# Attention and Fourier mixing on one core: first loads shared out anew, copies of values by engines in place of transfers, and a new order of work

## The chip, the cores and the metric

The kernel runs on one core of a Trainium2 chip. The core has a matrix engine (TensorE, PE in the profile), three engines for elementwise work (VectorE or DVE, ScalarE or ACT, GpSimd or POOL) and SyncE (SP), which only issues transfers. Transfers are issued by SyncE and ScalarE on two hardware queues, and by GpSimd on a software queue, which can change a type from fp32 to fp16 on the way. The metric is device time in microseconds: 255.69 us, the median of three runs (255.09, 255.69 and 258.91).

## The reference

Attention over four batches, eight heads, 768 positions, 64 columns, with a distance penalty and a narrow mask, then Fourier mixing over positions and columns, a normalisation and two feed-forward products:

```python
scores = q @ k.T / 8 - slope[h] * dist           # keys 0..7 for all, else 0 <= i - j < 96
a = exp(scores - max) / sum
x = (a @ v), heads side by side                  # 4 x 768 x 512
u = x + real(fft(fft(x, axis=1), axis=2))
un = (u - mean(u)) / sqrt(var(u) + 1e-6)
out = u + max(un @ w_ch1, 0) @ w_ch2             # 512 -> 2048 -> 512
```

## The kernel before

**Batches and stages.** Each batch goes through four stages. Attention works on pairs of heads: pairs 0 to 3 belong to batch 0, 4 to 7 to batch 1, and so on. q and k of a pair are turned so that the head's columns lie on partitions (`trans`, TensorE, for batches 0 and 1; transposing transfers, `trans_dma`, for 2 and 3). Scores come in three groups of blocks (`score`), ScalarE takes the exponential, the weighted sums with the values follow (`av`), and VectorE divides by the row sum (`norm`). In batches 0 and 1 the distance penalty is a product as well: `score` first multiplies the distance table `dist_sb` (in the tile `misc`) by a scaled identity, L676, and adds q·k on top, L690. In batches 2 and 3 a mask `mk` is multiplied in afterwards, L725. Folds of x, products with tables (`y_unit`, `u_unit`) and a sum make u; each batch has three units of two row groups, c = 0 to 11, and each unit is normalised (`centre`), transposed (`nt_unit`), and sent through the products with w_ch1 (`ph_unit`, L1292) and w_ch2 (`pg_unit`, `pg_units`, L1325 and L1434).

**Two kinds of copies.** A block's scores need the keys of its own and of the block before, and key blocks 1 to 4 exist a second time with the first 16 rows of each half taken from block 0, the global keys. `swap` in `trans` makes that copy for batches 0 and 1 (the tile kB, which lies in `mk`; L630 and L631). The values have the same: vB holds value blocks 1 to 4 with the first rows taken from block 0. `v_back`, L731 to L748, makes vB for each pair. For batches 0 and 1 it is a copy of the whole, 128x528, and two copies of 16 rows, 16x528, on GpSimd or VectorE. For batches 2 and 3 (`b >= FB`) it is three transfers on SyncE's queue: rows 32 to 127 (L739) and twice rows 0 to 31 (L741). There are eight pairs in batches 2 and 3, so 24 such transfers. `av` waits for vB.

**First loads.** Pair 0 (`load_qk` with `n in pl.HW`) is read in four halves as fp32 by the hardware queues, 192 KB each, into the tile u, and cast to fp16 into hT by ScalarE or VectorE (L544, L546). Everything else of q, k and v comes by GpSimd's queue with the cast on the way. GpSimd's queue, and the hardware queues together, hold eight transfers in flight each; a ninth issue waits until the first has landed. `dma_const` reads the identity, 32 KB, and the distance table, 320 KB, on a hardware queue.

**The order.** The order of the work on every engine is written out by hand as lists of names, `Plan.ORDER`, L197: A, M, H and G are units of TensorE work (attention, mixing, first and second feed-forward product), `A9.0` is the first follow-up of unit A9, and `T.17` is the seventeenth piece that no unit makes, transfers for the most part. `Plan.run` goes through the lists, and the semaphores follow from what each piece reads and writes. An engine works strictly down its list: what stands behind a waiting piece waits too. So the order before of the first loads is: ScalarE's queue takes the distance table, both halves of k, the first half of q; SyncE's takes the second half of q and the identity; GpSimd's takes q and k of pairs 2 and 3, then values, then pair 1.

Of the kernel before, what the change touches and what calls it, by code (L numbers as in the profile page):

```python
# [14 lines left out]
P = 128  # L15


class Ring(str):

    k = 0  # L20
# [4 lines left out]
class Plan:  # L25
# [112 lines left out]
    def move(self, go=False):  # L138
# [3 lines left out]
        both = [h[2] for k, h in act if k != "AQ"]  # L142
        each = sum(both) * (self.MIX if len(both) > 1 else 1.0) / 1000.0
        rate = {k: h[2] / 1000.0 if k == "AQ" else each for k, h in act}
# [31 lines left out]
    def unit_start(self, unit):  # L176
# [7 lines left out]
        if not there:  # L184
# [7 lines left out]
    AQ = ()  # L192
# [14 lines left out]
        ),  # L207
        "ACT": (
# [9 lines left out]
        ),  # L218
        "DVE": (
# [11 lines left out]
        ),  # L231
        "POOL": (
# [5 lines left out]
        ),  # L238
# [5 lines left out]
        ),  # L244
    }

# [60 lines left out]
def kernel(  # L307
# [22 lines left out]
    FB = 2  # L330
# [1402 lines left out]
```

## Time and profile before

| | |
|---|---|
| runs | 255.09, 255.69, 258.91 us |
| the profiled execution | 253.6 us, its span 251.5 us |
| mean granted TensorE clock | 0.991 of full speed |
| busy: TensorE, VectorE, ScalarE, GpSimd | 233.2, 196.0, 129.9, 105.5 us |
| GpSimd's queue (q0) | 66,176 packets, 17.06 MB |
| SyncE's queue (q1) | 30,128 packets, 13.15 MB |
| ScalarE's queue (q10) | 3,712 packets, 3.28 MB |

The views: *windows* give, for stretches of the span, its length, then for each engine busy microseconds and instructions, the granted clock (PEclk), the share of transfer engines and GB/s. *Timeline* rows have the start, the busy time, the engine, the line, the operation, the tile written and read, and in brackets how long the engine had been idle and what ended that. `ACTq` or `SPq` is an instruction of the engine's sequencer, here one that issues a transfer. Views of a line or tile give minimum, median and maximum duration in nanoseconds and the first and last start. A TensorE row's busy time has modelled ends, so units that run into each other look full even where they wait a little.

### The profile page before, as it was taken

To read this page: it belongs to the slowest core of one execution; us is meant where nothing else is said; L and a number is where in the kernel's file an instruction comes from. 1 tells how busy PE (TensorE), PEld (TensorE's weight loads), DVE (VectorE), ACT (ScalarE), POOL (GpSimd) and SP (SyncE) were. 2 spreads that over 40 slices of the span, in tenths; PEclk is the share of its full clock that TensorE was granted. 3 is DMA by queue.
4 is the path that set the end of the run, shared out by engine and by line. 5 is a ranking of instruction groups with operands and counts; after the bars stand their busy time and mean duration, and the time that the engine had idled before them with its cause. 6 is when DMAs were issued, how large, how long until landed. Compare 5 with 4: busy or idle time off the path is not lost.

```text
span 251.5 us, 7622 instructions
## 1 busy us (share of the span) xinstructions
PE 233.2 (93%) x3251; PEld 192.0 (76%) x3251; DVE 196.0 (78%) x425; ACT 129.9 (52%) x216; POOL 105.5 (42%) x151
## 2 busy tenths in 40 slices
PE   7468698899999999999999999999999999999994
PEld 2356586678756766788887978899889888888883
DVE  1255899987976669999998977789978987575683
ACT  2039568665559665754646568484436603204300
POOL 8689996999124922929801002220030160001210
PEclk9889999999999999999999999999999999999998
DMA  7999999999999998999999990230651222030412
GB/s 177 177 156 136 164 166 234 199 198 145 173 183 192 182 178 174 128 196 119 135 192 244 232 165 5 86 89 0 169 209 44 42 42 86 0 44 1 169 67 100
DMA packets 100049, 33.96 MB, mean 135 GB/s; under 512 B 86736, under 2 KB 96592, under 8 KB 100016
## 3 DMA queue, kind: packets, MB, share of 16 engines
q0 software_dynamic: 66176, 17.06, 69.6%
q1 hardware_dynamic: 30128, 13.15, 24.8%
q10 hardware_dynamic: 3712, 3.28, 4.8%
q8 instruction: 25, 0.41, 0.7%
q14 instruction: 8, 0.07, 0.1%
HBM read 31.48 MB, written 8.65 MB: 160 GB/s over the span
## 4 chain that ended last, share of the span: by engine, by line
PE 57%; DVE 6%; SPq 2%; DMA 2%; POOL 1%; issue 1%; ACT 0%; DVEq 0%; POOLq 0%
PE ph L1292 25%; PE pgD L1434 12%; PE pgA L1434 9%; PE pg L1325 4%; PE pav L774 2%; PE sc L684 2%; PE py L1057 2%; DMA out_dram<-u 2%; PE pu L1145 1%; DVE u L1452 1%; DVE u L1197 1%; SPq L578 1%; DVE sb L1410 1%; SPq L741 0%; SPq L739 0%
## 5 line engine op out<-in xcount | busy, mean ns | idle before, releaser
L1292 PE MATMUL ph<-unT,w 128*128 128x256 f16 x768 | 94.3, 273 | 0.6 <-ACT hT L1298 0.5
L1292 PEld LDWEIGHTS <-w 128*128 128x128 f16 x768 | 73.7, 98 | 11.7 <-issue 0.9
L1298 ACT ACTIVATE hT<-ph 128x512 f16<-128x512 f32 x71 | 41.4, 596 | 59.5 <-PE ph L1292 59.4
L1238 POOL TENSOR_SCALAR sm<-sm 128x2 f32<-128x2 f32 x12 | 4.0, 331 | 93.9 <-ACT un L1231 93.5
L1434 PEld LDWEIGHTS <-hT 128*128 128x128 f16 x320 | 30.9, 98 | 4.0
L710 ACT ACTIVATE er<-sc 128x1024 f16<-128x1024 f32 (+1 forms) x24 | 22.7, 953 | 11.9 <-PE sc L684 8.6
L713 ACT ACTIVATE ex<-sc 128x1024 f16<-128x1024 f32 (+1 forms) x24 | 21.7, 967 | 13.4 <-PE sc L690 13.4
L1299 DVE TENSOR_SCALAR hT<-ph 128x512 f16<-128x512 f32 x25 | 16.9, 685 | 9.7 <-PE ph L1292 9.6
L1452 DVE SCALAR_TENSOR_TENSOR u<-pgA,sm,u 128x256 f32<-128x256 f32 (+1 forms) x30 | 17.0, 567 | 5.5 <-PE pgA L1434 5.0
L725 DVE TENSOR_TENSOR ex<-er,mk 128x1024 f16<-128x1024 f16 (+1 forms) x24 | 15.0, 640 | 5.1 <-ACT er L710 4.5
L499 POOL DMA_DIRECT2D qk<-in_k_dram x16 | 13.6, 867 | 10.3 <-DMA qkT<-qk 9.1
L1452 DVE SCALAR_TENSOR_TENSOR u<-pgD,sm,u 128x512 f32<-128x512 f32 (+1 forms) x21 | 15.1, 721 | 3.0 <-PE pgD L1434 1.8
L1325 PE MATMUL pg<-w,hT 128*128 128x512 f16 x64 | 15.6, 379 | 0.0
L1231 ACT ACTIVATE un<-un 128x512 f16<-128x512 f16 x24 | 14.9, 625 | 0.1
L774 PE MATMUL pav<-v,ex 128*128 128x65 f16 x224 | 13.2, 193 | 1.5 <-DVE qkT L623 1.0
L1071 ACT ACTIVATE zy<-py 128x512 f16<-128x512 f32 (+1 forms) x13 | 10.2, 793 | 8.4 <-PE py L1057 6.7
L774 PEld LDWEIGHTS <-ex 128*128 128x128 f16 x352 | 12.3, 97 | 2.7 <-issue 1.3
L499 POOL DMA_DIRECT2D qk<-in_q_dram x16 | 13.6, 857 | 0.6 <-DMA v<-in_v_dram 0.5
L786 DVE TENSOR_TENSOR x<-pav,rc 128x384 f16<-128x384 f32 x24 | 12.6, 554 | 0.6
L1057 PE MATMUL py<-t,ww 128*128 128x256 f16 x80 | 11.0, 272 | 0.5 <-ACT ex L713 0.5
L1239 POOL TENSOR_TENSOR sm<-sm,mhalf 128x2 f32<-128x2 f32 x12 | 10.6, 887 | 1.0
L676 PE MATMUL sc<-misc 64*64 64x512 f16 (+1 forms) x96 | 9.4, 372 | 1.8 <-ACT qkT L626 0.8
(166 smaller groups left out, 467.9 us busy)
## 6 DMA issues: line engine op xcount, KB each, us to landing
w<-in_moe_w_ch_dram POOLq DMA_DIRECT2D x8, 512.0 KB, 9.3
out_dram<-u SPq DMA_DIRECT2D x15, 256.0 KB, 2.6
v<-in_v_dram POOLq DMA_DIRECT2D x12, 192.0 KB, 7.1
qk<-in_k_dram POOLq DMA_DIRECT2D x16, 96.0 KB, 5.2
qk<-in_q_dram POOLq DMA_DIRECT2D x16, 96.0 KB, 5.4
xr<-xd SPq DMA_DIRECT2D x3, 512.0 KB, 5.2
xd<-x ACTq DMA_DIRECT2D x2, 768.0 KB
vB<-v SPq DMA_DIRECT2D x8, 99.0 KB, 3.6
```

Of the source, the lines that this page charges most:

```text
L499: nc.gpsimd.dma_start(qk16[n][:, w, :, h], src[b, h0 + h].rearrange("(i m) d -> m i d", m=P))
L710: A(mine(), cut(pa), AF.Exp, 0.0, 0.125)
L713: A(cut(expst[hp][:, :, g * 512:g * 512 + (384 if g == 2 else 512)]), cut(pa), AF.Exp, 0.0, 0.125)
L725: VT(o, mine(), m, op=ALU.mult)
L774: nc.tensor.matmul(o[:, s * 65:(s + 1) * 65], lhsT, w, start=(a == 0), stop=(a == len(ops) - 1), skip_group_check=True)
L1057: nc.tensor.matmul(o, lhsT, rhs, start=(x == 0), stop=(x == len(ops) - 1))
L1292: nc.tensor.matmul(ph[:, a * CH:(a + 1) * CH].rearrange("p (x m) -> p x m", x=2), W1[0][:, d, jb * P:(jb + 1) * P], UNT[c][:, :, d, :], st ...
L1298: pl.later([("ACT", act(512), lambda: A(dst, ph, AF.Relu)), ("DVE", dve(512), lambda: V.tensor_scalar_max(dst, ph, 0.0))], [], e, [("h", c ...
L1299: ("DVE", dve(512), lambda: V.tensor_scalar_max(dst, ph, 0.0))],
L1325: nc.tensor.matmul(pg, HT[c][:, jb, t * P:(t + 1) * P], W2[0][:, jb, :], start=(jb == 0), stop=(jb == NJ - 1))
L1434: nc.tensor.matmul(o, lhs(j), rhs(j), start=(first and j == 0), stop=(j == NK - 1), skip_group_check=True)
L1452: V.scalar_tensor_tensor(o, x, r(t), acc, op0=ALU.mult, op1=ALU.add)
```

## The change

1. **First halves.** The order puts the second half of k and the first half of q on SyncE's queue; ScalarE's takes the second half of q, the identity and the first half of k. ScalarE casts three halves and VectorE one (before: two and two).
2. **Distance table.** `dma_const` gets a third way for the table, GpSimd's queue, and the order uses it: fifth there, behind q and k of pairs 2 and 3. Behind it come k of pair 1 and the values of pairs 0 and 2.
3. **vB of batches 2 and 3.** The transfers are gone. One whole copy and one copy of 32 rows, on GpSimd (pairs 1 and 2 of batch 2, all four of batch 3) or VectorE (pairs 0 and 3 of batch 2). `av` no longer waits for the second and third transfer.
4. **Order made anew.** All five lists are new. Among what moves until the first unit is transposed: TensorE starts with the scores of pair 0 in place of pair 2's. The key copies of pairs 0, 2 and 5 go from VectorE to GpSimd, those of pairs 3 and 1 the other way; that of pair 0 stands behind GpSimd's thirteenth load, that of pair 2 behind two loads more. Two of the three copies of spread rows (L1129) go from VectorE to ScalarE (L1127), and the copy of pair 6's transposed q and k from ScalarE (L626) to VectorE (L623). VectorE's division for the last pairs of batch 1 comes after the first unit's transposition, and so do two more of the weighted sums of batch 1 on TensorE. On SyncE's queue the table for the masks stands behind a transposing transfer of batch 2 in place of one of the vB transfers.

The planner's own estimates in `move` and the costs in `later` change as well; with the order written out, they decide nothing of the program that is built.

```diff
@@ Plan.move
-        both = [h[2] for k, h in act if k != "AQ"]
+        sw = any(k == "SW" for k, h in act)
+        both = [h[2] for k, h in act if k != "AQ" or sw]
...
-        rate = {k: h[2] / 1000.0 if k == "AQ" else each for k, h in act}
+        rate = {k: h[2] / 1000.0 if k == "AQ" and not sw else each for k, h in act}
@@ Plan.ORDER, the heads of the lists
         "PE": (
-            "A0 A1 A5 A15 A9 A8 A19 A20 A18 A4 A6 A2 A3 A14 A13 A10 A12
+            "A0 A5 A1 A15 A3 A2 A4 A7 A20 A6 A9 A8 A10 A19 A11 A12 A14
...
         "ACT": (
-            "T.9 T.6 T.4 T.0 T.7 T.5 A9.0 A19.0 A20.0 A18.0 A8.0 A4.0
+            "T.2 T.8 T.4 T.7 T.1 T.5 A3.0 A4.0 A2.0 A7.0 A20.0 A8.0
...
         "POOL": (
-            "T.11 T.12 T.20 T.19 T.16 T.21 T.13 T.23 T.36 T.18 T.14 T.32 T.15 T.17 T.33 A15.0
+            "T.11 T.12 T.19 T.20 T.9 T.14 T.15 T.16 T.18 T.13 T.17 T.21 T.22 A1.0 T.36 T.31 T.30 A5.0
...
         "SP": (
-            "T.2 T.8 T.131 T.35 T.10
+            "T.6 T.0 T.136 T.35 T.10
@@ v_back
-        if b >= FB:
-            low, high = slice(0, 32), slice(32, P)
-            pl.later([("SP", 0.66, lambda: nc.sync.dma_start(vB[hp][high], v16[b % 2][high, h, 1:NS - 1, :]))], after, 0.0, [("vB", b, hp)], lat=0.5, dma=(192, 1.56))
-            for x in range(2):
-                pl.later([("SP", 0.66, lambda x=x: nc.sync.dma_start(vB[hp][low, x], head(low)[:, x]))], after, 0.0, [("vC", b, hp, x)], lat=0.5, dma=(128, 0.6))
-            return
+        rows = (slice(0, 32),) if b >= FB else (slice(0, GR), slice(64, 64 + GR))
 
         def cp(eng):
             eng.tensor_copy(vB[hp], v16[b % 2][:, h, 1:NS - 1, :])
-            for r in (slice(0, GR), slice(64, 64 + GR)):
+            for r in rows:
                 eng.tensor_copy(vB[hp][r], head(r))
@@ av
-            needs = [...] + VN(b, [hp]) + [("vB", b, hp)] + [("vC", b, hp, z) for z in range(2 * (b >= FB))]
+            needs = [...] + VN(b, [hp]) + [("vB", b, hp)]
@@ dma_const
         ways = both(lambda on: on.dma_start(dst, src.ap()), 0.48 if soon else 0.42)
+        if tok == ("c", "dist"):
+            ways = ways + [("POOL", 0.66, lambda: nc.gpsimd.dma_start(dst, src.ap()))]
```

More of the change, by code (lines that the diff above doesn't have):

```diff
@@ L198 @@
         "PE": (
[8 rows of a table removed]
[8 rows of a table added]
         ),
         "ACT": (
[9 rows of a table removed]
[9 rows of a table added]
         ),
         "DVE": (
[11 rows of a table removed]
[11 rows of a table added]
         ),
         "POOL": (
[5 rows of a table removed]
[5 rows of a table added]
         ),
         "SP": (
[4 rows of a table removed]
+            "T.6 T.0 T.136 T.35 T.10 T.127 T.133 T.128 T.130 T.134 T.91 G7.1 G3.1 T.137 T.131 T.100 T.101 T.176 T.185 T.205 T.102 T.177 T.206 T.182 T.34 "
+            "T.140 T.186 T.211 T.212 T.183 T.149 T.179 T.180 T.150 T.151 T.223 T.189 T.222 T.229 T.228 T.198 T.199 T.239 T.200 T.240 T.246 T.245 T.256 "
+            "T.258 T.257 "
         ),
@@ L736, in v_back @@
         after = VN(b, [hp]) + [("sets",)] + [("avh", b - 1, hp)] * (b > 0)
-        if b >= FB:
-            low, high = slice(0, 32), slice(32, P)
-            pl.later([("SP", 0.66, lambda: nc.sync.dma_start(vB[hp][high], v16[b % 2][high, h, 1:NS - 1, :]))], after, 0.0, [("vB", b, hp)], lat=0.5, dma=(192, 1.56))
-            for x in range(2):
-                pl.later([("SP", 0.66, lambda x=x: nc.sync.dma_start(vB[hp][low, x], head(low)[:, x]))], after, 0.0, [("vC", b, hp, x)], lat=0.5, dma=(128, 0.6))
-            return
+        rows = (slice(0, 32),) if b >= FB else (slice(0, GR), slice(64, 64 + GR))
         def cp(eng):
             eng.tensor_copy(vB[hp], v16[b % 2][:, h, 1:NS - 1, :])
-            for r in (slice(0, GR), slice(64, 64 + GR)):
+            for r in rows:
                 eng.tensor_copy(vB[hp][r], head(r))
-        pl.later([("POOL", 1.8, lambda: cp(nc.gpsimd)), ("DVE", 0.9, lambda: cp(V))], after, 0.0, [("vB", b, hp)], rank=RA(b))
+        pl.later([("POOL", 0.6 + 0.6 * len(rows), lambda: cp(nc.gpsimd)), ("DVE", 0.3 + 0.3 * len(rows), lambda: cp(V))], after, 0.0, [("vB", b, hp)], rank=RA(b))
     def v_global(b):
@@ L807, in av @@
         for x in range(1 if b else 2):
-            needs = [("ex", b, hp, g) for g in ((0, 1, 2) if b else (1, 2) if x else (0, 1))] + VN(b, [hp]) + [("vB", b, hp)] + [("vC", b, hp, z) for z in range(2 * (b >= FB))]
+            needs = [("ex", b, hp, g) for g in ((0, 1, 2) if b else (1, 2) if x else (0, 1))] + VN(b, [hp]) + [("vB", b, hp)]
             needs += [("av", b - 1, g, 0) for g in range(HP) if b > FB] + [("qkT", HP + g) for g in range(2) if b == 1] + [("av", b, hp, 0)] * x
```

70 rows, old and new, of the table ORDER are left out of this document.

## The prediction

> **What bounds the kernel now.** I read the windows first, cut where the work changes its kind, then the transfers of the first 15 us, then the timeline of the first 25 us.
>
> ```profile
> core 0: us, PE busy (x) PEld busy (x) DVE busy (x) ACT busy (x) POOL busy (x), PEclk, DMA share, GB/s
> 0.00:6.33 6.33, 4.88 (x15) 1.75 (x15) 0.86 (x2) 1.81 (x2) 5.25 (x11) 1.00 0.80 178
> 6.33:10.02 3.69, 0.00 (x1) 0.00 (x0) 0.41 (x3) 0.52 (x1) 1.92 (x6) 1.00 1.63 185
> 10.02:14.59 4.57, 3.99 (x73) 3.58 (x73) 2.84 (x11) 0.00 (x0) 3.33 (x5) 0.64 2.11 165
> 14.59:20.00 5.41, 3.82 (x130) 2.91 (x128) 1.36 (x4) 3.24 (x4) 5.35 (x8) 0.99 2.51 149
> 20.00:30.00 10.00, 7.91 (x226) 6.27 (x221) 7.42 (x17) 7.16 (x9) 9.16 (x14) 1.00 2.27 153
> 30.00:45.80 15.80, 12.60 (x318) 9.77 (x318) 15.37 (x44) 12.00 (x19) 13.61 (x21) 1.00 1.51 196
> 45.80:56.20 10.40, 9.67 (x192) 7.93 (x192) 8.98 (x21) 7.25 (x11) 10.00 (x17) 1.00 1.47 196
> 56.20:80.00 23.80, 23.11 (x276) 16.89 (x275) 19.88 (x43) 15.01 (x29) 10.48 (x16) 1.00 1.48 175
> 80.00:245.00 165.00, 164.37 (x2011) 140.66 (x2010) 136.67 (x283) 82.93 (x145) 46.38 (x61) 1.00 0.71 115
> ```
>
> From 80 to 245 us TensorE stands still for 0.63 us of 165, and from 56.2 to 80 for 0.69. Its work is the same after the change, so time is gained or lost only where TensorE idles: before 56.2 us, and in a tail whose order is unchanged. Before 10.02 us there is no useful work at all (the x15 are warm-up products); between 30 and 45.8 us VectorE, busy 15.37 of 15.8, is the bound.
>
> ```profile
> GB/s 0 0 0 0 55 123 298 292 285 324 337 329 270 193 160 152 210 210 199 191 182 176 185 165 179 180 178 164 159 157 156 173 176 167 157 155 159 171 176 159
> ...
> hT<-in_k_dram POOLq DMA_DIRECT2D x3, 192.0 KB, 8.6
> ...
> u<-in_k_dram ACTq DMA_DIRECT2D x2, 192.0 KB, 6.4
> misc<-distm ACTq DMA_DIRECT2D x1, 320.0 KB, 3.4
> ...
> ident<-idm SPq DMA_DIRECT2D x1, 32.0 KB
> ```
>
> The transfers of the first 15 us: bandwidth in 40 slices of 0.375 us, then issues with their size and median time to landing. It runs at some 300 GB/s until 4.9 us, then 155 to 210, for good. Summed, 2313 × 0.375 = 867 KB have moved by 4.9 us.
>
> ```profile
> 4.71 0.37 DVE L546 CAST hT<-u 128x384 f16<-128x384 f32 x1 [3.31 <-DMA u<-in_q_dram]
> ...
> 5.46 0.52 ACT L544 ACTIVATE hT<-u 128x384 f16<-128x384 f32 x1 [1.33 <-DMA u<-in_k_dram]
> ...
> 8.19 0.52 ACT L544 ACTIVATE hT<-u 128x384 f16<-128x384 f32 x1 [2.21 <-DMA u<-in_k_dram]
> 9.61 0.36 DVE L546 CAST hT<-u 128x384 f16<-128x384 f32 x1 [4.52 <-DMA u<-in_q_dram]
> ...
> 10.02 2.56 PE L599 MATMUL pt<-ident,hT 128*64 128x128 f16 x48 [3.69 <-DVE hT L546]
> 10.07 0.75 POOL L482 DMA_DIRECT2D v<-in_v_dram  x1 [1.81 <-DMA hT<-in_q_dram]
> ...
> 11.18 0.83 POOL L539 DMA_DIRECT2D hT<-in_k_dram  x1 [0.37 <-DMA hT<-in_k_dram]
> ...
> 13.17 1.06 PE L599 MATMUL pt<-ident,hT 128*64 128x128 f16 x16 [0.58 <-DMA hT<-in_q_dram]
> ...
> 14.59 0.39 PE L676 MATMUL sc<-misc 64*64 64x384 f16 x4
> ...
> 15.20 0.81 ACT L713 ACTIVATE ex<-sc 128x768 f16<-128x768 f32 x1 [6.49 <-PE sc L690]
> ...
> 16.07 0.63 POOL L630 COPY mk<-qkT 128x512 f16<-128x512 f16 x1
> 16.76 0.29 POOL L631 COPY mk<-qkT 128x128 f16<-128x128 f16 x1
> ...
> 17.57 7.72 ACT L713 ACTIVATE ex<-sc 128x1024 f16<-128x1024 f32 x9 [1.56 <-PE sc L690]
> ```
>
> The last q half, fourth on ScalarE's queue behind the distance table, is cast at 9.61; then TensorE starts. GpSimd's own loads land at 10.07 (its first: the ninth issue waits for it), 11.18 (second) and 13.17 (pair 3 complete): (13.17 − 10.07) / 3 = 1.03 us for each 192 KB. The first scores come at 14.59, and the exponentials run without a break only from 17.57.
>
> **The change, part by part.** *First halves.* The hardware queues now carry four halves of 192 KB and 32 KB of identity, 800 KB in place of 1,120. By the sum above 867 KB had moved by 4.9 us, and 736 KB (table, identity, two halves) had landed at 5.46. I take the last half at 5.7 us and cast at 6.3; bounds are 5.0 (the bytes moved) and 8.2 (the third landing of now). So the first transposes run near 6.4, against 10.02. This alone brings nothing: TensorE's next unit is pair 2, from GpSimd's queue.
>
> *Table on GpSimd's queue.* It is the fifth transfer there, behind the 768 KB of pairs 2 and 3. Until pair 3 lands, 320 KB less have to move; at 175 GB/s that is 1.8 us, so pair 3 lands at 13.17 − 1.8 = 11.4. The 320 KB of the table come next, again 1.8 us: 13.2. Bounds: 12.5 at the 300 GB/s of the early slices, 14.9 if nothing is won from the lighter queues (13.17 + 1.03 × 320/192). No score can start without it. Behind it in the queue stand k of pair 1 and all the values, later by as much.
>
> *Copy of the keys of pair 0 to GpSimd.* It now stands behind GpSimd's thirteenth transfer, which, by the same rule of eight in flight as at 10.07, waits for the fifth, the table: 13.2 + 0.83 of issue + 0.63 + 0.29 of copies = 14.95. So the first exponential comes at about 15.2, as now, but three of pair 0 follow one another (nine take 7.72, so 0.86 each, to 17.8), and pair 2's keys, copied after two more issues and some constants (an estimated 0.4), are there at 14.95 + 1.66 + 0.4 + 0.92 = 17.9, when they end. Now one exponential runs early and the stream starts at 17.57, as if at 17.57 − 0.81 = 16.76. The lead is about 1.5 us.
>
> *Order made anew.* Its effect on VectorE until the first unit is transposed:
>
> ```profile
> L1129 DVE COPY u<-px 128x1024 f32<-128x1024 f32 x2 | 2.4, 1217 | 0.1
> L786 DVE TENSOR_TENSOR tt<-pav,rc 128x384 f16<-128x384 f32 x2 | 1.0, 552 | 0.0
> L623 DVE COPY qkT<-pt 128x1536 f16<-128x1536 f16 x5 | 4.8, 953 | 5.0 <-PE pt L599 4.9
> L1073 DVE CAST zy<-py 128x512 f16<-128x512 f32 x3 | 2.0, 687 | 0.3 <-PE py L1057 0.3
> ```
>
> Two spread copies go to ScalarE (−2.4), the division of one pair of batch 1 comes later (−1.1), one half's cast goes (−0.4), and two key copies come for three that go (an estimated −0.4, as that cast). In come one copy of transposed q, k (+0.95) and, net, one result copy (+0.7), and two small scaled copies of the fold (an estimated 0.2 each, half of the cast). Net −2.2 us. VectorE is the bound for part of this stretch only (idle 0.43 us of 15.8, then 1.42 of 10.4), so I count half: 1.1. The feed-forward products start 1.5 + 1.1 = 2.6 us earlier. But two more weighted sums of batch 1 are left over for later:
>
> ```profile
> 117.64 1.33 PE pav L774 x44
> ```
>
> 44 products are two such units: 1.33 us that TensorE still owes. Net gain 2.6 − 1.3 = 1.3 us.
>
> *Copies of values for batches 2 and 3.* Eight sets, each now three transfers on SyncE's queue, become two copies each, six sets on GpSimd, two on VectorE.
>
> ```profile
> L745 POOL COPY vB<-v x6: 622/640/783, 25.6 to 53.8; 128x528 f16<-128x528 f16 x6
> L745 DVE COPY vB<-v x2: 290/498/707, 21.3 to 24.8; 128x528 f16<-128x528 f16 x2
> L747 POOL COPY vB<-v x12: 617/620/837, 26.3 to 55.2; 16x528 f16<-16x528 f16 x12
> ...
> L741 SPq DMA_DIRECT2D vB<-v x16: 585/614/1454, 66.5 to 167.5; - x16
> L739 SPq DMA_DIRECT2D vB<-v x8: 601/616/907, 100.6 to 142.4; - x8
> ```
>
> GpSimd gains 6 × (0.64 + 0.62) = 7.6 us where it is busy 46.38 of 165; VectorE 2 × 2 × 0.29 to 0.71, 1.2 to 2.8 us, where it has 28.3 idle; SyncE loses 24 × 0.61 = 14.7 us of issuing. I cost it at nothing: TensorE waits 0.63 us there in all. What is queued behind a GpSimd copy that waits for its values are loads for batch 3 and the scaling of a unit's rows (the pow); who waits for that is VectorE's scaled sum, then a bank of TensorE. If that cover is gone, a late landing is the price: a load behind seven others comes 8 × 1.03 = 8.2 us after its issue, and a copy could hold GpSimd's queue for so long. Below nothing I put 0.6, TensorE's whole idle time. Nothing is nearest to the row of 80 to 245 us, where GpSimd and VectorE both have room.
>
> The Trainium skill (SBUF — State Buffer, Who interferes with whom) says that a VectorE copy in a two-port mode and a GpSimd operation shut each other out for the whole instruction. The VectorE copy above agrees in kind: 290 ns at best, 707 at worst. By that rule each collision costs the later one the other's 0.62 to 0.64 us; the sum without it is the one below.
>
> *Sum.* Profiled execution: 253.6 us, span 251.5, so 2.1 us lie around it. 253.6 − 1.3 = 252.3; the median of the runs shown is 255.69, 2.1 above the profiled one, so the forecast is 252.3 + 2.1 = **254.4 us**. All of VectorE's relief (1.1 more) or none (1.1 less), with the start's lead 0.4 either way, make 252.9 to 255.9.
>
> **The rivals.** *Faster, 0.15.* The table lands at 12.5 and TensorE is not slowed: the clock of 0.64 between 10.02 and 14.59 follows 3.69 us of idling. With the first transposes at 6.4 and the next near 9.4 the gap is under 3 us. If the clock stays full, two units of 24 transposes at half speed gain some 0.6 each (48 in 2.56 us now). With all of VectorE's relief: 1.3 + 0.7 + 1.2 + 1.1 = 4.3, so 255.69 − 4.3 = 251.4. The Trainium skill (TensorE: Matmul & The Clock Gate, Part 1) has the array drop to half its rate after about 3.4 us without work; the trace agrees (3.69 us, then 0.64), and by that rule the new gap would just pass.
>
> *Table late, slower, 0.17.* It lands at 14.9 or after. Then pair 0's keys are copied at 16.65, the stream starts at 16.9, no lead is left, and the 1.33 owed stays: 255.69 + 1.3 = 257.0. It decides from a landing after 14.7. For it: GpSimd's loads move at half the rate of the early slices. Against: 320 KB less stand ahead.
>
> *GpSimd's copies get in VectorE's way, slower, 0.13.* If each of the twelve new GpSimd copies stretches a VectorE operation as the copy above was, from 290 to 707 ns, 12 × 0.42 = 5.0 us of VectorE go, between 100 and 200 us. It decides where the stretched operation empties a bank for TensorE. Against it are 28.3 us of idle VectorE; if half reaches TensorE, 254.4 + 2.5 = 256.9, if all does, 259.4.
>
> *Nothing changes, 0.05.* The order gives back what the start gains: 255.7.
>
> **How the numbers follow.** The forecast's own case has 0.50, 252.9 to 255.9. Range 251.4 to 257.5: it takes in the faster case's centre and both slower ones', and leaves out about 0.2. Two per cent, 5.1 us, is about what a measurement of this kernel can tell from no change, its runs lying 3.8 us apart. Faster by it (under 250.6) needs more than all gains above: 0.07. Slower (over 260.8) needs both slower cases at their worst: 0.08. Within: 0.85.
>
> **What would show it.** Right: first transposes at 6 to 8 us, the first product with the table at 12.5 to 14, exponentials without a break from about 15.2, first feed-forward products near 53.6 in place of 56.2, TensorE's idle time from there to 245 still under 2 us. Wrong: a table after 14.7, GpSimd's key copy after 16, or new TensorE idle between 100 and 200 us that ends with a GpSimd copy or a VectorE sum.

## The result and the profile after

The kernel after takes 252.09 us, the median of 20 runs (250.35 to 254.78); the kernel before took 255.81 in 20 runs beside them (253.84 to 258.91). The ratio is 0.9859, 95% interval 0.9832 to 0.9886: 3.6 us, 1.4%, faster. The forecast was 254.4 with a range down to 251.4. Medians in this document are over all runs of a kernel, while ratios leave out runs in a slower state, to which half of the runs of e12_after_more and the profiled executions of e1_before_again and e9_copies_tables_late below belong, so the two can differ.

The profiled execution of the kernel after took 251.96 us, its span 250.2. The windows of it, cut as in the prediction (length, busy us and instructions of each engine, granted clock, share of the transfer engines, GB/s):

```profile
core 0: us, PE busy (x) PEld busy (x) DVE busy (x) ACT busy (x) POOL busy (x), PEclk, DMA share, GB/s
...
6.33:10.02 3.69, 2.26 (x43) 1.77 (x43) 0.00 (x0) 0.52 (x1) 2.58 (x4) 1.00 1.73 202
10.02:14.59 4.57, 1.93 (x40) 1.24 (x37) 3.99 (x10) 0.00 (x0) 3.11 (x5) 1.00 2.17 181
14.59:20.00 5.41, 4.73 (x118) 3.73 (x119) 2.57 (x5) 3.63 (x5) 5.29 (x12) 0.68 2.43 142
20.00:30.00 10.00, 7.51 (x200) 6.00 (x197) 9.52 (x22) 7.14 (x9) 9.73 (x15) 0.93 1.62 169
30.00:45.80 15.80, 14.98 (x330) 11.76 (x328) 14.96 (x40) 10.23 (x15) 10.56 (x17) 0.94 1.49 199
45.80:56.20 10.40, 10.22 (x218) 7.88 (x217) 6.61 (x16) 9.51 (x16) 9.74 (x17) 1.00 1.44 149
56.20:80.00 23.80, 23.80 (x296) 17.86 (x293) 20.94 (x47) 11.24 (x25) 14.52 (x19) 1.00 1.66 169
80.00:243.80 163.80, 162.45 (x1995) 139.09 (x1994) 137.41 (x287) 88.28 (x155) 50.34 (x65) 1.00 0.71 114
```

TensorE works from 6.33 us on, but between 10.02 and 20 us it does less than before, 158 products in place of 203, so that by 20 us both kernels have done just over 200. The difference is from 30 to 56.2 us: idle 0.82 + 0.18 = 1.0 us of 26.2, where it was 3.20 + 0.73 = 3.9. It gains 0.69 in the stretch to 80 us as well, and after that it is idle for 1.35 us (before: 0.63).

The timeline of the first 20 us, with the steps that the prediction timed:

```profile
6.33 0.52 PE L599 MATMUL pt<-ident,hT 128*64 128x128 f16 x6
7.08 0.52 ACT L544 ACTIVATE hT<-u 128x384 f16<-128x384 f32 x1 [1.32 <-DMA u<-in_k_dram]
7.66 1.11 PE L599 MATMUL pt<-ident,hT 128*64 128x128 f16 x18 [0.80 <-ACT hT L544]
...
13.21 0.41 PE L676 MATMUL sc<-misc 64*64 64x512 f16 x4 [1.16 <-DMA misc<-distm]
...
14.87 0.29 POOL L631 COPY mk<-qkT 128x128 f16<-128x128 f16 x1
15.21 0.31 PE L690 MATMUL sc<-qkT,mk 64*64 64x128 f16 x2 [1.54 <-POOL mk L631]
...
15.90 1.02 ACT L713 ACTIVATE ex<-sc 128x1024 f16<-128x1024 f32 x1 [8.29 <-PE sc L690]
...
17.39 4.41 ACT L713 ACTIVATE ex<-sc 128x768 f16<-128x768 f32 x5 [0.47 <-PE sc L690]
```

The table lands at 13.21 and TensorE waits for it, the key copy of pair 0 ends at 14.87 + 0.29 = 15.16 and TensorE waits 1.54 us for that. The stream of exponentials starts at 17.39 where it had started at 17.57.

Two milestones carry the rest of this document: the first fold (`fold_pe`, tile pf, the products that turn x of batch 0 into its folded halves) and the first feed-forward product (tile ph). The views of the two tiles give minimum, median and maximum in ns, then the first and last start in us. Kernel before, pf, then ph:

```profile
L965 PE MATMUL pf<-x,ident x32: 219/219/229, 34.7 to 39.6; 128*128 128x128 f16 x32
```

```profile
L1292 PE MATMUL ph<-unT,w x768: 269/273/283, 56.2 to 237.7; 128*128 128x256 f16 x192
```

Kernel after:

```profile
L960 PE MATMUL pf<-x,ident x32: 217/219/229, 32.2 to 37.6; 128*128 128x128 f16 x32
```

```profile
L1287 PE MATMUL ph<-unT,w x768: 269/273/283, 53.4 to 236.0; 128*128 128x256 f16 x192
```

From fold to feed-forward both take as long: 56.2 − 34.7 = 21.5 and 53.4 − 32.2 = 21.2. Of the lead of 2.8 us, 2.5 are there when the folds begin. From the first feed-forward product to the end of the span it was 251.5 − 56.2 = 195.3 us and is 250.2 − 53.4 = 196.8, so 1.5 are given back; around the span lie 1.8 us in place of 2.1. Between the two profiled executions that makes −2.8 + 1.5 − 0.3 = −1.6 us, near the forecast's −1.3. Between the medians it is 3.7, because the profiled execution of before (253.6) lies below all 20 of these runs of its kernel, and that of after at the median of its own.

### The profile page after: what moved, and what is told of

It is laid out like the page before. It is cut to its first block, busy times and chain, and to the rows that moved or that the text cites. A ratio compares the mean times of both kernels' runs of the same rounds, so it can differ in the third digit from the quotient of the medians.

```text
span 250.2 us, 7615 instructions
## 1 busy us (share of the span) xinstructions
PE 235.1 (94%) x3251; PEld 193.0 (77%) x3251; DVE 199.0 (80%) x430; ACT 132.9 (53%) x222; POOL 111.1 (44%) x157
## 3 DMA queue, kind: packets, MB, share of 16 engines
q0 software_dynamic: 66256, 17.39, 69.3%
## 4 chain that ended last, share of the span: by engine, by line
PE 79%; DMA 6%; DVE 6%; ACT 3%; POOL 2%; issue 1%; ACTq 0%; POOLq 0%
PE ph L1287 34%; PE pgD L1429 13%; PE pgA L1429 10%; PE pg L1320 6%; PE pav L769 4%; DMA misc<-distm 3%; PE py L1052 3%; DMA unT<-un 3%; PE pu L1140 3%; PE sc L684 3%; ACT ex L713 2%; PE sc L676 2%; POOL hT L539 1%; PE sc L690 1%; DVE qkT L623 1%
## 5 line engine op out<-in xcount | busy, mean ns | idle before, releaser
L1293 ACT ACTIVATE hT<-ph 128x512 f16<-128x512 f32 x74 | 43.3, 596 | 65.8 <-PE ph L1287 65.6
L710 ACT ACTIVATE er<-sc 128x1024 f16<-128x1024 f32 (+1 forms) x24 | 22.5, 952 | 10.2 <-PE sc L684 8.3
L1294 DVE TENSOR_SCALAR hT<-ph 128x512 f16<-128x512 f32 x22 | 15.1, 688 | 6.7 <-PE ph L1287 6.5
L725 DVE TENSOR_TENSOR ex<-er,mk 128x1024 f16<-128x1024 f16 (+1 forms) x24 | 16.2, 686 | 4.4 <-ACT er L710 4.4
L1447 DVE SCALAR_TENSOR_TENSOR u<-pgD,sm,u 128x512 f32<-128x512 f32 (+1 forms) x21 | 15.2, 723 | 4.3 <-PE pgD L1429 4.0
L1320 PE MATMUL pg<-w,hT 128*128 128x512 f16 x64 | 15.8, 379 | 0.0
L769 PEld LDWEIGHTS <-ex 128*128 128x128 f16 x352 | 13.3, 99 | 2.1 <-issue 1.3
L1304 POOL DMA_INDIRECT out_dram<-u,back x4 | 4.7, 1184 | 22.3 <-DVE u L1447 22.0
L769 PE MATMUL pav<-v,ex 128*128 128x65 f16 x224 | 13.9, 196 | 0.1
L676 PE MATMUL sc<-misc 64*64 64x512 f16 (+1 forms) x96 | 10.8, 422 | 2.8 <-DMA misc<-distm 1.2
L1217 ACT ACTIVATE un<-u,sm 128x512 f16<-128x512 f32 x17 | 11.9, 714 | 1.7 <-DVE sm L1184 1.7
L623 DVE COPY qkT<-pt 128x1536 f16<-128x1536 f16 (+1 forms) x8 | 6.6, 850 | 6.8 <-PE pt L599 6.8
```

The lines of the kernel that those rows point to most:

```text
L676: nc.tensor.matmul(o, sid[r, 2 * hp + s, r], m, start=True, stop=False, skip_group_check=True, tile_position=(64 * s, 64 * t))
L710: A(mine(), cut(pa), AF.Exp, 0.0, 0.125)
L725: VT(o, mine(), m, op=ALU.mult)
L769: nc.tensor.matmul(o[:, s * 65:(s + 1) * 65], lhsT, w, start=(a == 0), stop=(a == len(ops) - 1), skip_group_check=True)
L1293: pl.later([("ACT", act(512), lambda: A(dst, ph, AF.Relu)), ("DVE", dve(512), lambda: V.tensor_scalar_max(dst, ph, 0.0))], [], e, [("h", c ...
L1294: ("DVE", dve(512), lambda: V.tensor_scalar_max(dst, ph, 0.0))],
```

## The experiments

In the table, "before" is the median of the kernel before in the runs beside it, "fold" and "ph" are the first starts of the two tiles in the profiled execution, and the last column is the rest of the span behind ph.

| kernel | us (runs) | before | ratio, 95% interval | fold | ph | ph to end |
|---|---|---|---|---|---|---|
| before, the profile shown | | | | 34.7 | 56.2 | 195.3 |
| e1_before_again | 255.14 (12) | 254.73 | 0.9992, 0.9957 to 1.0026 | 35.3 | 57.9 | 196.0 |
| e2_start_only | 255.02 (12) | 254.73 | 0.9993, 0.9957 to 1.0028 | 36.1 | 57.9 | 195.0 |
| e5_copies_only | 255.76 (12) | 254.96 | 1.0048, 1.0010 to 1.0087 | 37.4 | 59.8 | 195.6 |
| e9_copies_tables_late | 258.63 (6) | 254.85 | 1.0105, 1.0053 to 1.0157 | 35.0 | 56.4 | 201.2 |
| e14_copies_gate | 257.94 (6) | 255.18 | 1.0105, 1.0063 to 1.0146 | 34.9 | 56.1 | 200.1 |
| e10_before_warm | 255.20 (12) | 254.85 | 1.0015, 0.9977 to 1.0053 | 35.8 | 57.3 | 194.6 |
| e11_before_relief | 255.11 (12) | 254.85 | 1.0022, 0.9998 to 1.0046 | 36.1 | 58.5 | 194.2 |
| e13_fold_first | 258.19 (6) | 255.18 | 1.0123, 1.0083 to 1.0163 | 31.9 | 59.8 | 195.4 |
| after, the profile shown | 252.09 (20) | 255.81 | 0.9859, 0.9832 to 0.9886 | 32.2 | 53.4 | 196.8 |
| e16_after_again | 251.06 (6) | 255.83 | 0.9853, 0.9801 to 0.9905 | 31.6 | 53.0 | 196.3 |
| e4_old_start | 251.66 (6) | 254.73 | 0.9850, 0.9807 to 0.9892 | 32.3 | 53.8 | 196.3 |
| e6_table_hw | 251.03 (6) | 254.96 | 0.9864, 0.9815 to 0.9913 | 32.9 | 54.3 | 195.9 |
| e7_spread_dve | 252.03 (12) | 254.96 | 0.9897, 0.9863 to 0.9931 | 31.4 | 53.9 | 196.4 |
| e8_unT_earlier | 251.96 (12) | 254.96 | 0.9906, 0.9869 to 0.9943 | 32.4 | 53.9 | 196.9 |
| e15_fold_late | 252.68 (12) | 255.83 | 0.9869, 0.9834 to 0.9903 | 34.4 | 55.8 | 196.4 |
| e3_vb_transfers_back | 254.41 (6) | 254.73 | 0.9898, 0.9840 to 0.9957 | 31.2 | 52.6 | 200.1 |
| e12_after_more | 256.58 (12) | 254.85 | 0.9990, 0.9954 to 1.0026 | 31.4 | 52.9 | 201.2 |

**What one execution is worth.** The kernel before once more, with no edit, and the kernel after likewise:

> The kernel before, unchanged, as a run of its own: what its runs differ by from one to the next. If the profiled execution that the sum was made against (253.6 us) was an ordinary one, the median here is 253.6 to 254.5 and other profiles look like it. If that execution was a lucky one (theory: the base of the sum was off), the median is 255.5 to 256.0 and another profile shows a longer span than 251.5 us, with the extra time before 20 us, where the granted clock was 0.64 between 10.02 and 14.59.

> The kernel after, unchanged, in the same call: its own median beside e15_fold_late, and a second profile of it. If the first feed-forward product of the new order is steady, it lies between 52.5 and 54.5 us here too, where that of before lay between 56.1 and 59.8; time 0.986 of before.

The second profile of before has its ph at 57.9, that of after at 53.0. Two further kernels (e9, e14) leave all that runs ahead of the ph as it is in before: 56.4 and 56.1. So three of the four unedited openings lie at 56.1 to 56.4, and e1 stands apart. With small edits ahead of the ph (e2, e5, e10, e11) the old order lies from 57.3 to 59.8. The new one, in seven profiles of kernels that leave it as it is from 20 us to the ph (after, e16, e4, e6, e8, e3, e12), lies from 52.6 to 54.3, 53.4 in the mean.

Part of the scatter of the old order can be read off the timelines: TensorE stops with nothing to wait for that the profile shows. In the profiled execution of before it does so once, in the scores; in e1, and then in e5, one of several stops lies in the second fold:

```profile
44.36 0.24 PE L690 MATMUL sc<-qkT 64*64 64x128 f16 x1 [1.35 <-issue]
```

```profile
39.81 0.49 PE L965 MATMUL pf<-x,ident 128*128 128x128 f16 x6 [0.99 <-issue]
```

```profile
41.99 0.38 PE L961 MATMUL pf<-x,ident 128*128 128x128 f16 x4 [1.14 <-issue]
```

These two need 22.6 and 22.4 us from fold to ph, where before, e9 and e14 need 21.2 to 21.5. All nine profiles of the old order, the edited ones included, have such stops of 0.3 us or more ahead of the ph: 1.1 to 1.4 us in before, e9 and e14, 2.2 in e1, 3.4 in e5, 0.6 to 2.3 in the others. The seven of the new order named above have none. So 1.35 of the 3.9 us that TensorE idled from 30 to 56.2 us in before are such a stop. What causes the stops, and whether their absence is a part of the gain, was not tried.

**The start alone, and all but the start.**

```diff
 e2_start_only: the kernel before
-ACT "T.9 T.6 T.4 T.0 T.7 T.5 ..."   SP "T.2 T.8 ..."   POOL "T.11 T.12 T.20 T.19 T.16 ..."
+ACT "T.2 T.8 T.4 T.7 T.1 T.5 ..."   SP "T.6 T.0 ..."   POOL "T.11 T.12 T.20 T.19 T.9 T.16 ..."
 e4_old_start: the kernel after
-ACT "T.2 T.8 T.4 T.7 T.1 T.5 ..."   SP "T.6 T.0 ..."   POOL "... T.20 T.9 T.14 ..."
+ACT "T.9 T.6 T.4 T.0 T.7 T.5 ..."   SP "T.2 T.8 ..."   POOL "... T.20 T.14 ..."
 e6_table_hw: the kernel after
-SP "T.6 T.0 T.136 ..."   POOL "... T.20 T.9 T.14 ..."
+SP "T.6 T.0 T.9 T.136 ..."   POOL "... T.20 T.14 ..."
```

> The kernel before with the new first loads alone (halves on both hardware queues, the table fifth on GpSimd's queue); the order behind them and the transfers of values as before. By the prediction's own pieces the start's lead of 1.5 us needs the new order too (pair 0's scores come third here), so 0 to 1.5 us faster: 254.3 to 255.8. Theory 'the start was undersized' (the idle TensorE until 10 us, and the slow clock behind it, cost more than counted): 252 to 253.3. Theory 'the values' transfers cost': no gain here, 255.8.

> The kernel after with the first loads of before (table and halves on the hardware queues as there); the new order and the copies stay. Prediction's pieces (start 1.5, the rest -0.2): 253.6. Theory 'the start is the whole gain': 255.5 to 256. Theory 'order and copies are the gain': 252.1 to 252.8.

> The kernel after with the distance table third on SyncE's hardware queue in place of fifth on GpSimd's; all else as after. By the prediction's sum the table's place sets the first score (13.2) and with it a lead: a table at 8 us would bring the first exponential forward by 1 us or more, 251.0 or less. Theory 'the start has no weight, VectorE's work from 20 us on sets the first feed-forward product': as after within 0.5 us, first feed-forward product at 53 to 54 us.

All three say that the start carries nothing. With the new start alone the kernel before stays where it was (0.9993), although its first transposes come at 6.7 us. With the old start the kernel after stays as fast as it is (0.9850), although its first transposes come at 10.1 and its first score at 15.2. The table on a hardware queue changes nothing either (0.9864). Whatever the start, the first fold comes at a time that goes with the order: 32.3, 32.9 and 31.6 to 32.2 in the new one, 36.1 in the old one.

**VectorE's relief, put back and alone.**

```diff
 e7_spread_dve: the kernel after
-ACT "... T.72 M0.1 A25.1 M1.0 M4.0 A35.0 A28.0 A38.0 M5.0 M2.1 ..."   DVE "... M1.1 T.81 ... T.83 M2.0 ..."
+ACT "... T.72 M0.1 A25.1 M1.0 A35.0 A28.0 A38.0 M2.1 ..."   DVE "... M1.1 M4.0 T.81 ... T.83 M5.0 M2.0 ..."
 e11_before_relief: the kernel before
-DVE "... M5.0 M2.0 M2.1 M3.0 M4.0 M7.0 ..."   ACT "... A28.0 A32.0 ... M3.1 A36.0 ..."
+DVE "... M2.0 M2.1 M3.0 M7.0 ..."   ACT "... A28.0 M5.0 A32.0 ... M3.1 M4.0 A36.0 ..."
```

> The kernel after with the spread copies of the first two units on VectorE again (two copies of 1.2 us, out of ScalarE's list, into VectorE's at about 39 and 44 us). The prediction counted VectorE's relief half: 1.2 us slower, first feed-forward product at 54.5. Theory 'VectorE is the bound all the way to that product': 2.4 us slower, product at 55.8, 254.4. Theory 'VectorE's relief is hidden': no change.

> The kernel before with the two spread copies of 1.2 us taken from VectorE and given to ScalarE, the largest part of the relief that the prediction counted half. Prediction: 1.2 us faster, 253.7. Theory 'VectorE is the bound from 30 us to the first feed-forward product': 2.4 faster, 252.5. Theory 'a chain of waits through TensorE, VectorE and ScalarE, not VectorE's load' (e7_spread_dve, where these copies put back cost nothing): 0 to 0.5 faster.

In the new order, with the two copies on VectorE, the way from fold to ph takes 53.9 − 31.4 = 22.5 us, against 21.2 to 21.5 in the seven profiles above: 1.0 to 1.3 us more, about half of the 2.4 that the copies take. The trace of e7 does not settle whose they are: TensorE waits 0.89 us at 45.29 for one of the copies, and it stops 0.91 us at 39.34 with nothing to wait for. The ratio, 0.9897, is 0.4% above that of after, with intervals that overlap. In the old order the same relief is worth nothing: fold to ph takes 22.4 us and the ratio is 1.0022. So the spread copies did not bound the kernel before.

**The folds.**

```diff
 e13_fold_first: the kernel before
-PE "... A39 A21 A40 A22 A25 A26 M1 A37 ..."   ACT "... A39.0 A40.0 T.72 A25.1 T.77 M1.1 ..."   DVE "... A26.1 M1.0 ..."
+PE "... A21 A22 M1 A39 A40 A25 A26 A37 ..."   ACT "... T.72 T.77 M1.1 A39.0 A40.0 A25.1 ..."   DVE "... M1.0 A26.1 ..."
 e15_fold_late: the kernel after
-PE "... A23 M0 A24 A25 A34 M1 ... A26 ..."   ACT "... M0.1 A25.1 ..."   DVE "... M0.0 ... A26.1 ..."
+PE "... A23 A25 A26 M0 A24 A34 M1 ..."   ACT "... A25.1 M0.1 ..."   DVE "... A26.1 M0.0 ..."
```

> The kernel before with one piece of the new order alone: on TensorE the first fold (M1) goes ahead of two scores and two transpositions of batch 1 (A39, A40, A25, A26) that stood before it, and what follows them on ScalarE and VectorE moves along. In the kernel after the first fold ends at 34.1 us, in the kernel before at 36.6. Theory 'the gain is batch 0's chain through the folds going ahead of batch 1's work on TensorE': first feed-forward product 2 us or more earlier than the 57 to 58 us of the runs of before, 252.5 to 253.5. Theory 'no single move does it, the new order as a whole gives it': 0 to 0.7 us faster. VectorE's load is the same as before, so the prediction's own reckoning gives no change.

> The kernel after with one piece of the old order put back: two transpositions of batch 1 (A25, A26) stand ahead of the first fold again, as they do in the kernel before, with their copies on ScalarE and VectorE ahead of what follows the fold. Theory 'batch 0's folds ahead of batch 1's transpositions is a large piece of the gain': first feed-forward product 1.5 to 2.5 us later (55 to 56 us), 253.5 to 254.5. Theory 'no single piece decides': less than 0.5 us.

e13 is a miss: the first fold starts at 31.9, but the second ends only at 43.3, since scores and transpositions of batch 1 now stand between the two, and 3 us are lost. Its first fold also waits 0.81 us, until 33.01, for rows of x from VectorE, so TensorE's list alone did not hold the fold back. e15 is the better trial. Two transpositions of batch 1 ahead of the first fold, with their copies, are enough to bring the new order's fold to where the old order has it:

```profile
L960 PE MATMUL pf<-x,ident x32: 219/219/230, 34.4 to 39.3; 128*128 128x128 f16 x32
```

```profile
L1287 PE MATMUL ph<-unT,w x768: 269/273/283, 55.8 to 238.0; 128*128 128x256 f16 x192
```

The ph is 2.8 us later than in e16, and the median 252.68 − 251.06 = 1.6 us longer in runs beside each other (ratios 0.9869 and 0.9853, whose intervals overlap). So this piece is worth 1.6 us by the medians and 0.4 by the ratios, which is less than half of the gain: e15 comes to its ph about as late as the old order and still takes 0.987 of the time of before. (Its profiled execution, 253.97 us, is the longest but one of its twelve.) No other piece of the order was tied to the gain.

**TensorE's clock in the old opening.**

```diff
 e10_before_warm: the kernel before
-    PZ = 15
+    PZ = 30
```

> The kernel before with 30 warm-up products in place of 15, so that TensorE is busy through its wait for the first loads (6.3 to 10.0 us). Theory 'before passes TensorE's slow clock on to the first feed-forward product': the granted clock between 10 and 15 us is 1.0 in place of 0.64 to 0.70, mean clock 0.99 or more in most runs, the first feed-forward product near 56 us, 253.5 or less. Theory 'the lateness in typical runs has other causes' (order, code loading): clock better, time as before, 254.9.

Windows of e10 (TensorE alone), 10 to 46 us:

```profile
10.02:14.59 4.57, 3.56 (x110) 1.00 2.14 166
14.59:20.00 5.41, 3.76 (x115) 1.00 2.64 156
20.00:30.00 10.00, 7.42 (x218) 1.00 2.44 163
30.00:45.80 15.80, 14.19 (x320) 0.89 1.51 199
```

The slow clock is gone from the start (before: 0.64) and comes between 30 and 45.8 us; the fold starts at 35.8 and the time is as before. In steps of 1 us it lies from 32 to 36, just ahead of the fold, so it was moved and not taken away, and this run does not tell what it costs. The runs in which the mean granted clock was 0.997 or more do: 14 of the kernel before have a median of 253.8 us, six of the kernel after, not all taken side by side, 250.9. Some 3.0 us of the gain are there without any slow clock to speak of.

**The copies of values.**

```diff
 e5, e9 and e14: the kernel before, with v_back and av of the kernel after
-SP "T.2 T.8 T.131 T.35 T.10 T.135 T.141 T.144 ..."   and the 24 names of vB and vC
+SP e5:  "T.2 T.8 T.35 T.10 T.135 T.141 T.144 ..."
+SP e9:  "T.2 T.8 T.135 T.35 T.10 T.141 T.144 ..."
+SP e14: "T.2 T.8 T.144 T.35 T.10 T.135 T.141 ..."
+POOL "... T.92 T.132 T.129 T.123 T.126 ... M17.11 T.180 T.183 T.186 T.189 ..."
 e3_vb_transfers_back: the kernel after, three transfers for each pair again
+SP "... T.100 T.123 T.126 T.125 T.101 T.124 ... T.140 T.172 ... T.180 T.175 T.150 T.173 T.174 ..."
```

> The kernel before with GpSimd's copies of values in place of the 24 transfers and nothing else (all eight sets on GpSimd: batch 2's four from about 90 us, batch 3's four from about 125 us, both in stretches where GpSimd stood idle). Prediction (copies cost and bring nothing): ratio 1.000, 254.7. Theory 'the transfers' removal is the missing 2.4 us': ratio 0.990 to 0.992, 252.3. Theory 'it is the order before the first feed-forward product': as the prediction, except for what lies around the span, 2.1 us with the transfers and 1.8 us without them in all runs so far, so 0.3 us faster, ratio 0.999; the first feed-forward product as late as in the kernel before (56.2 to 57.9 us).

> Again the kernel before with engine copies of values in place of the 24 transfers. In e5_copies_only one of the transfers taken out had held back two loads of tables on SyncE's queue until 70 us, and without it they were issued in the first microseconds, among the first loads. Here they stand behind the first transposing transfer of batch 2, as in the kernel after. If the copies as such cost (GpSimd's copies in VectorE's way): 255.8 as in e5_copies_only. If they cost and bring nothing but the 0.3 us around the span: 254.5 to 254.8, ratio 0.999.

> Once more the kernel before with engine copies of values in place of the 24 transfers, now with SyncE's queue held back as in both kernels: the first piece there after the first loads waits until about 70 us (a transposing transfer of pair 11, as in the kernel after; in the kernel before one of the transfers now taken out did that, and in e5 and e9 its absence let tables or transposing transfers start earlier). If the slowness of e5 and e9 came from that: 254.5 to 254.9, ratio 0.998 to 1.000. If the copies themselves cost: 255.7 or more.

> The kernel after with the values of batches 2 and 3 made by three transfers on SyncE's queue for each pair again, in place of the two copies. Prediction (the copies cost and bring nothing): as after, 252.1, within 0.3. Rival (the 24 transfers held SyncE's queue, so the missing 2.4 us are theirs): 253.5 to 254.5, and TensorE idle between 100 and 200 us above the 1.35 us of after.

None of the four is a clean answer on the time, and the trace says why. In the kernel before, T.131 waits at the head of SyncE's queue until 66.5 us and holds back all behind it. With it gone the transposing transfers, the mask table or the masks come at other times: in e9 the first transposing transfer is issued at 59.2 and TensorE later waits for weights; in e14 the queue opens only at 71.2, the table for the masks is late, and ScalarE, which has products to empty behind the masks, waits for it. The waits of TensorE in e9 (60 to 90 us), of ScalarE in e14 (66 to 80 us), of TensorE in e3 (100 to 140 us), with total, times and longest:

```profile
PE pg L1321 <- DMA w<-in_moe_w_ch_dram: 3.9, 1, 3.9
```

```profile
ACT mk L1597 <- DMA distk<-distkm: 4.6, 1, 4.6
```

```profile
PE pav L777 <- DMA vB<-v: 3.4, 3, 2.8
```

The price of the copies themselves can be read within e5 and e14, instruction by instruction against the profile of before. VectorE's list is the same in all three. Just ahead of the copies (88 us of before) it runs 3.7 us late in e5 and in e14, in the middle of batch 3's copies (129 us of before) 6.0 and 6.9, and from 155 us to the end 3.9 and 4.7 (e9: 5.4 ahead of them, 6.1 at the end). What is lost meanwhile is mostly stretched operations of VectorE; the view of tile ww, kernel before and then e5 (minimum, median, maximum):

```profile
L865 DVE TENSOR_TENSOR ww<-eA x3: 675/682/682, 66.2 to 178.5; 128x1024 f16<-128x1024 f16 x3
```

```profile
L861 DVE TENSOR_TENSOR ww<-eA x3: 680/683/1105, 69.6 to 182.4; 128x1024 f16<-128x1024 f16 x3
```

One of the three meets the copies and takes 1105 ns for 682: 0.42 us. Most of the two or three microseconds so lost is made good before 155 us. In the span, and in the old order, the copies so cost 0.1, 0.7 and 1.0 us in the three profiles (e5, e9, e14). Around the span the removal of the transfers brings 0.3: the runs of kernels with the 24 transfers show 1.9 to 2.3 us there, those without them 1.7 to 1.9.

In the new order the transfers put back (e3) leave the ratio at 0.9898, two thirds of the gain; the rest is 0.4% of the time, with intervals that overlap.

**Two tries to beat the kernel after.**

```diff
 e8_unT_earlier: the kernel after
-PE "... A59 A58 H32 H33 G22 ..."   ACT "... A50.0 T.40 T.41 M17.7 H29.0 M17.3 M17.8 ..."
+PE "... A59 A58 G22 H32 H33 ..."   ACT "... A50.0 M17.7 M17.8 T.40 T.41 H29.0 M17.3 ..."
 e12_after_more: e8 and e6, and
-DVE "... T.202 A54.1 G16.0 T.99 T.204 ... A52.1 T.126 M20.0 ..."   POOL "... G15.1 T.169 ... T.155 T.112 T.164 ..."
+DVE "... T.202 A54.1 G16.0 T.204 ... A52.1 M20.0 ..."   POOL "... G15.1 T.126 T.99 T.112 T.169 ... T.155 T.164 ..."
```

> The kernel after with one wait taken out: TensorE stood 1.0 us at 119 us for the transposed rows of unit 4. Its casts go ahead of two mask tables on ScalarE (1.4 us earlier) and one group of second feed-forward products goes ahead of the unit's first one on TensorE. If that wait is worth its face value: 1.0 us faster than after, 251.1. If TensorE only waits later instead: as after, 252.1.

> The kernel after with three edits meant to beat it: the table on SyncE's hardware queue (e6_table_hw), the two moves of e8_unT_earlier, and between 95 and 118 us, where VectorE is busy 19.8 of 20 us, one copy of values (0.8 us) and one repack of rows (0.4 us) from VectorE to GpSimd, with a load of values issued earlier. If VectorE's load there sets the time (every run in the new order has lost the same by 120 us, however it began): 1.2 us faster than after, 250.9 or less. If not: 251 to 252.1.

Windows of TensorE from 100 to 140 us, kernel after and then e8:

```profile
100.00:120.00 20.00, 18.65 (x332) 1.00 1.92 148
120.00:140.00 20.00, 20.00 (x218) 1.00 1.04 223
```

```profile
100.00:120.00 20.00, 19.39 (x339) 1.00 1.88 150
120.00:140.00 20.00, 19.32 (x210) 1.00 1.02 225
```

e8 takes 0.7 us of idling from the first stretch and finds 0.7 in the next, so the wait had cover behind it. e12 gives the whole gain away (0.9990); its longest wait of TensorE shows the other side of the copies:

```profile
PE pav L769 <- POOL vB L742: 3.5, 1, 3.5
```

Two more pieces on GpSimd ahead of its loads, and a copy of values comes late with nothing to cover it. No kernel tried is faster than the kernel after by more than the intervals allow.

## Why the prediction was right and wrong

**Right: the steps of the start.** First transposes near 6.4, table 13.2, key copy done at 14.95: measured 6.33, 13.21 and 15.16. The first of these is in part luck: 6.4 was worked out from the last of the four halves, which is cast only at 7.08, and the six transposes at 6.33 read a half cast before. "This alone brings nothing" held (e2_start_only, 0.9993). The rival with a late table did not come about.

**Wrong: "The lead is about 1.5 us."** The first exponential came at 15.90 and the unbroken stream at 17.39, not 15.2. More than that, no lead reaches the fold: e4_old_start has its first score 2.0 us later than after and its fold at 32.3 in place of 32.2. The term is 0 to 0.7 (32.3 against 31.6 in e16), and nothing in the time.

**Wrong, and the step that failed most: "Order made anew. Its effect on VectorE until the first unit is transposed."** The prediction priced the order by VectorE's load alone: 2.2 us of relief, counted half, 1.1, which the 1.33 owed eat up again, so that the whole net gain was to come from the start. It is the other way round. With the start of before (e4_old_start) the kernel keeps its gain, 0.9850 of 254.73, 3.8 us, where those two terms make it 0.2 longer; the start alone brings nothing, and copies in place of transfers alone bring nothing. By elimination the order, with what the copies add to it, is worth the 3.6 us.

The term also took its relief from the wrong place. VectorE was called the bound for 30 to 45.8 us, but the two spread copies, the largest part of the relief, start at the end of that stretch and behind it, and the division comes only at 53.92:

```profile
L1129 DVE COPY u<-px x2: 1210/1217/1224, 45.7 to 49.3; 128x1024 f32<-128x1024 f32 x2
```

Between 30 and 45.8 us VectorE is as full after (14.96 of 15.8) as before (15.37), and the copies taken away in the old order bring nothing (e11_before_relief). Whether VectorE's load inside that stretch holds the kernel up was not tried.

What the order does instead is known in part. The first fold comes at 31.2 to 32.9 us in place of 34.7 to 35.3, and from there both orders need 21 to 23 us. TensorE's list in the kernel before has four units of batch 1 (A39, A40, A25, A26) between the transposition of pair 6 (A30) and the first fold; the new one has two (A37, A36). e15_fold_late shows what two of them are worth, 0.4 to 1.6 us. The rest of the gain stays without a piece of the order to its name; that the new order shows none of the old one's stops of TensorE is an open lead.

**Right by two errors: "The feed-forward products start 1.5 + 1.1 = 2.6 us earlier".** 2.8 in the profiles, 2.5 of them there at the folds, and none of it from the start. That the sums agree is luck.

**Mis-sized: the base of that sum.** All of it was made against one execution of before that was faster than the 20 runs beside those of the change (253.84 at best; in other sets of runs it went down to 252.14). Its ph, 56.2, is no exception. Against the mean of the three openings that agree, 56.2, the lead is 2.8 us; with e1 the mean is 56.7 and the lead 3.3. With 1.4 given back (from ph to the end 196.4 us in the mean of after, e16, e4, e6 and e8, 195.0 in that of before, e1, e2, e10 and e11) and 0.3 around the span, the profiles give 1.7 to 2.2 us of the 3.6; the other 1.4 to 1.9 are not placed.

**Right: "The 1.33 us that TensorE still owes".** 1.5 in the profiles, 1.4 in the means, and for the reason given: behind the ph stand 264 of the products with values (tile pav) in place of 221.

**Nearly right: the copies "at nothing".** 0.1 to 1.0 us in the span, in the old order, and 0.3 won around it, which the prediction held constant. In time the three kernels with copies alone are 0.5 to 1.1% slower, but with other transfers moved as well. The rival that GpSimd gets in VectorE's way had its mechanism and its size (0.42 us for each collision, predicted from the copy of 290 to 707 ns) and not its end: most of the loss is made up by 155 us. The Trainium skill (SBUF — State Buffer, Who interferes with whom) says that a VectorE instruction with two inputs in SBUF contends with a GpSimd instruction that reads SBUF. The row of ww, a sum of two parts of eA, agrees: 0.42 us longer beside a copy. "A late landing is the price" if the cover is gone: e12_after_more paid it, 3.5 us.

**Wrong: the faster rival's clock.** It did not stay full: 0.68 between 14.59 and 20 us. The kernel was faster without it.

## What to carry to other kernels

When one stage holds everything up, look for the first piece of work that the next stage needs, and for what stands ahead of it on the engine that makes it. Before load taken off the busiest engine is counted as time won, see whether it lies inside the stretch in which that engine is full: here most of it lay behind. Take a second and third profile of the kernel before, if they are to be had, before a sum of a few microseconds is made against one of them. When a transfer is deleted from a queue, ask what it was holding back.

## What the runs showed of the hardware

TensorE's granted clock fell without a long pause. In the kernel after it was 0.68 between 14.59 and 20 us, and TensorE's longest wait from its first transposition to 20 us was 1.54 us; in e10_before_warm, with TensorE busy through the start, it was 1.00 until 30 us and 0.89 between 30 and 45.8. The Trainium skill (TensorE: Matmul & The Clock Gate, Part 1) has the array fall back to half its rate after an idle window of about 3.4 us. The kernel before agrees with that (3.69 us idle, then 0.64); these two do not.

Without 24 of its transfers on SyncE's queue the program's time around the span is 0.3 us shorter (1.7 to 1.9 in place of 1.9 to 2.3), in the old order as in the new.
